# Padding small tables onto 512-byte lines, and moving four output stores from ScalarE's queue to SyncE's

## The chip, the cores and the metric

The kernel runs on one core of one Trainium2 chip. The metric is device time in microseconds (us). Five engines run their own instruction streams and meet at semaphores: TensorE (PE, matmuls; PEld is its weight load), VectorE (DVE), ScalarE (ACT), GpSimd (POOL) and SyncE (SP). SP, ACT and POOL can issue DMAs. In the profile SPq, ACTq and POOLq are the issuing instructions of these queues, and "Lnnn" is a line of the kernel's file.

## What is computed

The reference runs a recurrent retention layer (4 batches, 8 heads, 768 steps, head size 64) and feeds its output, seen as 3072 tokens of 512, to a two-layer network with a leaky ReLU whose slope is learned:

```python
for t in range(S):
    state = gamma[None, :, None, None] * state + np.einsum('bhd,bhe->bhde', k[:, :, t], v[:, :, t])
    y[:, :, t] = scale * np.einsum('bhd,bhde->bhe', q[:, :, t], state)
x = y.transpose(0, 2, 1, 3).reshape(B * S, H * D)
h = x @ w_in                                             # 3072 x 2048
g = np.maximum(h, 0.0) + alpha * np.minimum(h, 0.0)
out = g @ w_out                                          # 3072 x 512, float32
```

## The kernel before, in words

**Units and blocks.** The retention is done in chunks of 128 steps. A unit `i` is two chunks and half of the heads; there are 24 units. Four units make a block of 512 tokens, and there are six blocks, 0 to 5. Block n's retention gives the tile `xT[n]`; then `ffn1(n)` (L335, 64 matmuls of 512 columns) gives `gt`, and `ffn2(n)` (L375, 64 matmuls) gives the output.

**Life of a unit.** `load` (L118) brings k, q and v of the unit to SBUF, 256 KB each, on SP's queue, into tiles `ks`, `qs`, `vs`. `u_prep` multiplies k and q by decay factors from the table `tab` (L145, tile `kdq`) and casts v (L161, `vx`). For blocks 0 and 1 the transposed copy `kq` is made by PE and ACT (`u_turn`, L175 and L184); from block 2 on it is made by a transposing DMA on SP's queue (`u_flip`, L165). `u_visit` has the state update (L204 on PE, L223, L227 on DVE, L228 on POOL), the scores (L245 on PE) and the mask (L258 on DVE). `u_out` (L280, L295 on PE) gives the unit's output, which ACT copies into `xT` (L315).

**The two layers.** For each of 16 slices of 128 hidden features, `ffn1` runs four matmuls into a PSUM tile `hps`; ACT makes `hm` from it (L345) and DVE makes `gt` (L346). For block 1 the first slice is done in two halves of 256 columns. `ffn2` ends, for each of four row groups, with ACT's copy of PSUM to `os_sb` (L384) and a store of 256 KB to `out` (L388), issued by ACT. With `parts=4`, as for block 0, all four row groups end in the last quarter of `ffn2`. PSUM tiles of all kinds share eight buffers, given in turn.

**Order.** The program's order is written out by hand (`manual_schedule`): each engine runs its instructions in the order in which they stand in the code, and the generators of `ffn1` and `ffn2` are advanced with `tick` between steps of the units. Around the change the code reads as follows: `ffn2(0)` is advanced between the visits of units 4 to 7, `u_out(7)` stands between its second and third row group, then come the twelve loads of block 2 (units 8 to 11), then `ffn1(1)`, and inside it, for each unit i of block 2, the preparation, `u_flip(8+i)` and the three loads of unit 12+i. So SP's queue has: loads of units 8 to 11, flip 8, loads of unit 12, flip 9, loads of unit 13, and so on. ACT's queue has: `os` copy and store of row groups 0 and 1, the two `xT` copies of unit 7, `os` copy and store of row groups 2 and 3, then the `hm` of `ffn1(1)`.

**Counters.** The DMAs issued by SP and ACT, in the program's order, take eight completion counters in turn; a DMA whose counter was last used by an earlier DMA carries a wait until that one has landed. The wait stands in the issuing engine's queue.

**Addresses.** SBUF tiles are laid one after another in the order of the code, each rounded up to 32 bytes per partition. In the compiled program `tab` starts 128 bytes past a line of 512 bytes; its 208 bytes, the 768 of `mi`, the 4 of `warm` and the 64 of `oma` leave every tile from `win` on (all of `ks`, `qs`, `vs`, `kdq`, `kq`, `xT`, `gt`, `os`) 192 bytes past a 512-byte line. `gmat`, `alpha` and `spin` start 96 bytes past one.

Of the kernel before, what the change touches and what calls it, by code (L numbers as in the profile page):

```python
# [9 lines left out]
FP = mybir.dt.float32  # L10
F16 = mybir.dt.float16
# [7 lines left out]
def kernel(  # L19
# [10 lines left out]
    nc = tc.nc  # L30
    B, H, S, D = q.shape
    d_model, d_ff = moe_w_in.shape
    NFT = d_ff // 128
# [13 lines left out]
    NTAB = 4 * H + NP + 16  # L47
# [24 lines left out]
    sbp = ctx.enter_context(tc.tile_pool(name="sbp", bufs=1, space=bass.MemoryType.SB))  # L72
    psp = ctx.enter_context(tc.tile_pool(name="psp", bufs=1, space=bass.MemoryType.PSUM))
    ctx.enter_context(tc.manual_schedule())

    tab = sbp.tile([128, NTAB], FP, tag="tab", name="tab")
    mi = sbp.tile([128, 384], F16, tag="mi", name="mi")
    ident = mi[:, 0:128]
    masku = mi[:, 128:384].rearrange("p (s i) -> p s i", s=2)
    gmat = sbp.tile([128, NP, 128], FP, tag="gmat", name="gmat")  # L80
    alpha_sb = sbp.tile([NFT, 128], FP, tag="alpha", name="alpha")
    spin = sbp.tile([128, 512], F16, tag="spin", name="spin")
    warm = sbp.tile([128, 1], FP, tag="warm", name="warm")
    oma_sb = sbp.tile([128, NFT], FP, tag="oma", name="oma")
    w_in_all = sbp.tile([128, 4, d_ff], F16, tag="win", name="win")
    w_out_all = sbp.tile([128, NFT, d_model], F16, tag="wout", name="wout")

# [5 lines left out]
    def ps(name, dt=FP, n=512):  # L93
        return psp.tile([128, n], dt, tag="ps", bufs=8, name=name)
# [15 lines left out]
    def load(u, names="kqv"):  # L110
        t = staged.setdefault(u, {})
        for nm in names:
            src = srcs[nm]
            st = sbp.tile([128, H * D], FP, tag=f"{nm}s", bufs=8, name=f"{nm}s{u}")
            j, g = divmod(u, 2)
            b, c = divmod(2 * j, NCH)
            t[nm] = st
            ins = nc.sync.dma_start(  # L118
                out=st.rearrange("p (h x) -> p h x", h=H // 2),
                in_=src[  # L120
                    b, H // 2 * g : H // 2 * g + H // 2, C * c : C * c + 2 * C, :
                ].rearrange("h (p s) d -> p h (s d)", s=2),
            )
            if held:
                tc.add_manual_dep(
                    ins.ins,
                    held.pop().ins.name,
                    mybir.DependencyInfo(
                        mybir.DependencyClass.Sync, mybir.DependencyReason.DATA
                    ),  # L130
                    reason="loads of the second block after the weights",
                )
# [195 lines left out]
    def ffn1(n, early=0):  # L328
        gt = sbp.tile([128, NFT, TB], F16, tag="gt", bufs=2, name=f"gt{n}")
        gts[n] = gt  # L330
        hpss = {}

        def product(ft, lo, hi, hps=range(4)):
            for hp in hps:
                nc.tensor.matmul(  # L335
                    out=hpss[ft][:, lo:hi],
                    lhsT=w_in_all[:, hp, 128 * ft : 128 * ft + 128],
                    rhs=xT[n][:, hp, lo:hi],
                    start=(hp == 0),
                    stop=(hp == 3),  # L340
                )
                if hp == 3 and hi == TB:
                    hpt = hpss.pop(ft)
                    hm = sbp.tile([128, TB], FP, tag="hm", bufs=3, name="hm")
                    nc.scalar.activation(out=hm, in_=hpt, func=RELU, bias=0.0, scale=-1.0)  # L345
                    nc.vector.scalar_tensor_tensor(  # L346
                        out=gt[:, ft, :],
                        in0=hm,
                        scalar=oma_sb[:, ft : ft + 1],
                        in1=hpt,  # L350
                        op0=MULT,
                        op1=ADD,
                    )
                yield

        for ft in range(early):
            hpss[ft] = ps("hps")
            yield from product(ft, 0, TB // 2)
            yield from product(ft, TB // 2, TB, range(2))
        for ft in range(early):  # L360
            yield from product(ft, TB // 2, TB, range(2, 4))
        for ft in range(early, NFT):
            hpss[ft] = ps("hps")
            yield from product(ft, 0, TB)

    def ffn2(n, parts=1):
        gt = gts.pop(n)
        opss = {}
        step = NFT // parts
        for f0 in range(0, NFT, step):  # L370
            for tq in range(UB):
                if f0 == 0:
                    opss[tq] = ps("ops")
                for ft in range(f0, f0 + step):
                    nc.tensor.matmul(  # L375
                        out=opss[tq],
                        lhsT=gt[:, ft, 128 * tq : 128 * tq + 128],
                        rhs=w_out_all[:, ft, :],
                        start=(ft == 0),
                        stop=(ft == NFT - 1),  # L380
                    )
                    if ft == NFT - 1:
                        os_sb = sbp.tile([128, d_model], FP, tag="os", bufs=6, name="os")
                        nc.scalar.activation(  # L384
                            out=os_sb, in_=opss[tq], func=COPY, bias=0.0, scale=1.0
                        )
                        row = TB * n + 128 * tq
                        nc.scalar.dma_start(out=out[row : row + 128, :], in_=os_sb)  # L388
                    yield

    def tick(gen, m):
# [14 lines left out]
    for lh in range(2):  # L406
        z = slice(64 * lh, 64 * lh + 64)
        nc.gpsimd.tensor_copy(
            out=gmat[z, :, z],
            in_=tab[z, 4 * H : 4 * H + NP].unsqueeze(2).to_broadcast([64, NP, 64]),  # L410
# [16 lines left out]
    def masked(i):  # L427
# [60 lines left out]
        out=aps[:, 0:NFT], in_=alpha_sb, identity=tab[0:NFT, NTAB - 16 : NTAB]  # L488
    )
    nc.vector.tensor_scalar(  # L490
        out=oma_sb, in0=aps[:, 0:NFT], scalar1=-1.0, scalar2=1.0, op0=MULT, op1=ADD
# [9 lines left out]
    gen = ffn1(0, early=4)  # L501
# [7 lines left out]
    u_scale(4, 0)  # L509
    for _ in gen:  # L510
        pass
    gen = ffn2(0, parts=4)

    def u_visit(i):
        st[i] = u_state(i)
# [39 lines left out]
        pass  # L555
    for u in range(2 * UB, 3 * UB):
        load(u)
    gen = ffn1(1, early=1)

    for n in range(1, NBLK):  # L560
        more = n + 1 < NBLK
        u0 = UB * (n + 1)
        if n > 1:
            gen = ffn1(n)
        if more:
            for i in range(UB):
                tick(gen, 14)
                u_prep(u0 + i, nc.gpsimd)
                u_flip(u0 + i)
                if u0 + i + UB < NU:  # L570
                    load(u0 + i + UB)
        for _ in gen:
            pass
        gen = ffn2(n)
        if more:
            for i in range(UB):
                u = u0 + i
                tick(gen, 2)
                if i:
                    u_out(u - 1)  # L580
                u_visit(u)
                tick(gen, 12)
            u_out(u0 + UB - 1)
        for _ in gen:
            pass
# [30 lines left out]
```

## Time and profile before

| | us |
|---|---|
| median of three runs (lowest, highest) | 222.0 (220.98, 224.34) |
| the profiled execution, its own time | 222.42 |
| its span, first to last instruction | 220.6 |
| TensorE busy in the span | 209.0 (95%) |
| VectorE, ScalarE, GpSimd busy | 119.6, 100.9, 83.1 |

The page cuts the span into 40 slices of 5.5 us; a digit is the busy share of a slice in tenths. The granted clock is 0.996 of full speed. A chain of waits follows the work back from the last instruction to what released it. Times of single rows are counted from the span's start.

### The profile page before, as it was taken

The numbers are of one execution on the slowest core, as the hardware profiler recorded it, in microseconds if no ns is written. First come the engines' busy times: TensorE is split into PE (matmuls) and PEld (weight loads), VectorE is DVE, ScalarE is ACT, GpSimd is POOL, SyncE is SP. The second block draws the span as 40 slices with busy tenths as digits, with TensorE's granted clock in tenths as the row PEclk, the third lists the DMA queues.
The fourth block names the chain that finished last, engine by engine and source line by source line (L and its number), as shares of the span: only waits on it lengthen the run. The fifth ranks groups of instructions, "written<-read, shape, count | busy, mean of one in ns | idle before, by whom it ended". The sixth has DMA issues, their size and how long they took to land.

```text
span 220.6 us, 4964 instructions
## 1 busy us (share of the span) xinstructions
PE 209.0 (95%) x2043; PEld 104.3 (47%) x2043; DVE 119.6 (54%) x195; ACT 100.9 (46%) x185; POOL 83.1 (38%) x107
## 2 busy tenths in 40 slices
PE   7998997899599999999999999999999999999992
PEld 3456543454344455444455444555444555444440
DVE  2674794655009954178846088554288642388000
ACT  2583873334329523376233466232567222666121
POOL 3487204941990042990013990112980331000000
PEclk9999999999999999999999999999999999999998
DMA  6999999978999961499911499811482002100111
GB/s 171 300 221 167 174 242 293 232 138 235 312 250 305 295 180 51 107 270 229 255 51 51 113 251 293 203 51 62 133 103 40 22 35 91 48 0 1 51 68 74
DMA packets 62935, 34.02 MB, mean 154 GB/s; under 512 B 18736, under 2 KB 59840, under 8 KB 62912
## 3 DMA queue, kind: packets, MB, share of 16 engines
q1 hardware_dynamic: 54912, 23.08, 45.5%
q0 software_dynamic: 4224, 4.19, 12.3%
q10 hardware_dynamic: 3776, 6.43, 8.1%
q8 instruction: 16, 0.26, 0.5%
q14 instruction: 7, 0.06, 0.1%
HBM read 27.40 MB, written 6.29 MB: 153 GB/s over the span
## 4 chain that ended last, share of the span: by engine, by line
PE 73%; DMA 12%; POOL 4%; SPq 3%; DVE 3%; issue 2%; ACT 1%; ACTq 0%; POOLq 0%; DVEq 0%
PE ops L375 35%; PE hps L335 28%; DMA qs<-in_q_dram 5%; DMA win<-in_moe_w_in_dram 4%; SPq L118 3%; PE yps L295 3%; DMA vs<-in_v_dram 3%; PE stp L204 2%; POOL tg L228 2%; POOL kdq L145 2%; PE yps L280 2%; PE sca L245 1%; DVE m L258 1%; POOL win L418 1%; PE scb L245 1%
## 5 line engine op out<-in xcount | busy, mean ns | idle before, releaser
L346 DVE SCALAR_TENSOR_TENSOR gt<-hm,oma,hps 128x512 f16<-128x512 f32 x96 | 69.1, 745 | 41.5 <-ACT hm L345 34.9
L375 PE MATMUL ops<-wout,gt 128*128 128x512 f16 x384 | 89.3, 380 | 0.0
L335 PE MATMUL hps<-xT,win 128*128 128x512 f16 (+1 forms) x404 | 84.6, 368 | 2.7 <-ACT xT L315 2.6
L345 ACT ACTIVATE hm<-hps 128x512 f32<-128x512 f32 x96 | 56.5, 597 | 24.3 <-PE hps L335 21.9
L335 PEld LDWEIGHTS <-win 128*128 128x128 f16 x404 | 39.4, 98 | 46.4 <-issue 3.3
L228 POOL TENSOR_TENSOR tg<-ss,gmat 128x256 f16<-128x256 f32 x32 | 23.2, 727 | 82.4 <-DVE ss L227 82.4
L375 PEld LDWEIGHTS <-gt 128*128 128x128 f16 x384 | 35.3, 98 | 39.9
L315 ACT ACTIVATE xT<-yps 128x256 f16<-128x256 f32 x48 | 18.5, 453 | 35.2 <-PE yps L295 28.4
L145 POOL TENSOR_TENSOR kdq<-qs,tab 128x512 f16<-128x512 f32 x24 | 25.4, 1059 | 17.4 <-DMA qs<-in_q_dram 17.4
L384 ACT ACTIVATE os<-ops 128x512 f32<-128x512 f32 x24 | 14.3, 597 | 37.5 <-PE ops L375 33.9
L227 DVE TENSOR_TENSOR ss<-tg,stp 128x256 f32<-128x256 f16 x32 | 13.2, 415 | 25.2 <-PE stp L204 25.2
L258 DVE TENSOR_TENSOR m<-sca,mi 128x512 f16<-128x512 f32 x24 | 16.4, 683 | 1.5 <-PE scb L245 1.1
L145 POOL TENSOR_TENSOR kdq<-ks,tab 128x512 f16<-128x512 f32 x16 | 16.7, 1045 | 0.0
L184 ACT ACTIVATE kq<-trb 128x512 f16<-128x512 f16 (+1 forms) x11 | 8.7, 790 | 16.9 <-PE trb L175 16.8
L258 DVE TENSOR_TENSOR m<-scb,mi 128x512 f16<-128x512 f32 x24 | 16.3, 680 | 0.0
L161 POOL CAST vx<-vs 128x512 f16<-128x512 f32 x20 | 12.7, 635 | 0.0
L204 PE MATMUL stp<-vx,kdq 64*64 64x128 f16 x320 | 9.7, 219 | 0.4 <-ACT vx L159 0.4
L295 PE MATMUL yps<-m,vx 64*64 64x128 f16 x384 | 10.0, 222 | 0.0
L100 PE MATMUL kps<-spin 128*128 128x512 f16 x22 | 8.5, 510 | 1.5 <-DVE spin L403 1.5
L245 PE MATMUL sca<-kq 64*64 64x128 f16 x192 | 9.7, 217 | 0.2
L245 PE MATMUL scb<-kq 64*64 64x128 f16 x192 | 9.7, 219 | 0.0
L223 DVE TENSOR_TENSOR tg<-stp,gmat 128x256 f16<-128x256 f32 x8 | 3.4, 423 | 11.0 <-PE stp L204 11.0
(25 smaller groups left out, 67.5 us busy)
## 6 DMA issues: line engine op xcount, KB each, us to landing
ks<-in_k_dram SPq DMA_DIRECT2D x24, 256.0 KB, 4.4
qs<-in_q_dram SPq DMA_DIRECT2D x24, 256.0 KB, 4.9
vs<-in_v_dram SPq DMA_DIRECT2D x24, 256.0 KB, 5.3
out_dram<-os ACTq DMA_DIRECT2D x24, 256.0 KB, 2.0
win<-in_moe_w_in_dram POOLq DMA_DIRECT2D x4, 512.0 KB, 7.1
wout<-in_moe_w_out_dram POOLq DMA_DIRECT2D x4, 512.0 KB, 9.1
kq<-kdq SPq DMA_TRANSPOSE x16, 4.5
mi<-mi_const ACTq DMA_DIRECT2D x1, 96.0 KB, 2.9
```

Of the source, the lines that this page charges most:

```text
L145: (eng or (nc.vector, nc.gpsimd)[a]).tensor_tensor(out=prepped[i][0][:, a], in0=staged[i]["kq"[a]].rearrange("p (h s d) -> p s h d", s=2, ...
L204: nc.tensor.matmul(out=stps[hf][64 * lh : 64 * lh + 64, 128 * r : 128 * r + 128], lhsT=kdu[z, 0, s, 2 * r + lh, :], rhs=vx[z, 2 * r : 2 * ...
L228: nc.gpsimd.tensor_tensor(out=tgs[u + 1][:, gs, :], in0=new, in1=gmat[:, gs, :], op=MULT)
L245: nc.tensor.matmul(out=scs[lh][z, c0 : c0 + 128], lhsT=kqv[y, 0, s, r, z], rhs=kqv[y, 1, :, r, z], start=True, stop=True,)
L258: nc.vector.tensor_tensor(out=m2, in0=scs[lh].rearrange("p (s r i) -> p s r i", s=2, r=2), in1=masku.unsqueeze(2).to_broadcast([128, 2, 2, ...
L295: nc.tensor.matmul(out=ypss[hf][64 * lh : 64 * lh + 64, 128 * r : 128 * r + 128], lhsT=vx[z, 2 * r + lh, s, :], rhs=m2s[lh][z, s, r, :], s ...
L315: nc.scalar.activation(out=xT[n][:, 2 * g : 2 * g + 2, c0 : c0 + C].rearrange("p a (i s) -> p a s i", s=2), in_=ypss[hf][:, 0:256].rearran ...
L335: nc.tensor.matmul(out=hpss[ft][:, lo:hi], lhsT=w_in_all[:, hp, 128 * ft : 128 * ft + 128], rhs=xT[n][:, hp, lo:hi], start=(hp == 0), stop ...
L345: nc.scalar.activation(out=hm, in_=hpt, func=RELU, bias=0.0, scale=-1.0)
L346: nc.vector.scalar_tensor_tensor(out=gt[:, ft, :], in0=hm, scalar=oma_sb[:, ft : ft + 1], in1=hpt, op0=MULT, op1=ADD,)
L375: nc.tensor.matmul(out=opss[tq], lhsT=gt[:, ft, 128 * tq : 128 * tq + 128], rhs=w_out_all[:, ft, :], start=(ft == 0), stop=(ft == NFT - 1),)
L384: nc.scalar.activation(out=os_sb, in_=opss[tq], func=COPY, bias=0.0, scale=1.0)
```

## The change

Four small tiles are allocated larger, and a slice of each is used as before: `tab` 52 to 96 floats a partition, `mi` 384 to 512 half floats, `warm` 1 to 64 floats, `oma` 16 to 64 floats. With these sizes `tab` ends on a 512-byte line, and each tile after it starts on one, except `oma`, which starts 256 bytes past a line.

The four stores of block 0 are no longer issued by ACT. `ffn2` keeps their rows and tiles in a list, and SP issues them, after the twelve loads of block 2 and ahead of flip 8. The stores of the other blocks stay with ACT.

```diff
-    tab = sbp.tile([128, NTAB], FP, tag="tab", name="tab")
-    mi = sbp.tile([128, 384], F16, tag="mi", name="mi")
+    tab = sbp.tile([128, 96], FP, tag="tab", name="tab")[:, 0:NTAB]
+    mi = sbp.tile([128, 512], F16, tag="mi", name="mi")[:, 0:384]
...
-    warm = sbp.tile([128, 1], FP, tag="warm", name="warm")
-    oma_sb = sbp.tile([128, NFT], FP, tag="oma", name="oma")
+    warm = sbp.tile([128, 64], FP, tag="warm", name="warm")[:, 0:1]
+    oma_sb = sbp.tile([128, 64], FP, tag="oma", name="oma")[:, 0:NFT]
...
-    def ffn2(n, parts=1):
+    def ffn2(n, parts=1, late=None):
...
                         row = TB * n + 128 * tq
-                        nc.scalar.dma_start(out=out[row : row + 128, :], in_=os_sb)
+                        if late is None:
+                            nc.scalar.dma_start(out=out[row : row + 128, :], in_=os_sb)
+                        else:
+                            late.append((row, os_sb))
...
-    gen = ffn2(0, parts=4)
+    stores = []
+    gen = ffn2(0, parts=4, late=stores)
...
     for u in range(2 * UB, 3 * UB):
         load(u)
+    for row, os_sb in stores:
+        nc.sync.dma_start(out=out[row : row + 128, :], in_=os_sb)
     gen = ffn1(1, early=1)
```

## The prediction, made before the change was run

> **What bounds the kernel now.** I read the page first, then the chain of waits in order of time, then the timelines of ACT, PE and SP where the chain leaves PE. The page says that PE is the bound:
>
> ```profile
> PE   7998997899599999999999999999999999999992
> ...
> DMA  6999999978999961499911499811482002100111
> ...
> PE 73%; DMA 12%; POOL 4%; SPq 3%; DVE 3%; issue 2%; ACT 1%; ACTq 0%; POOLq 0%; DVEq 0%
> ```
>
> After the first four slices the PE row has one true dip, the 5 in slice 11, which is 55 to 60.5 us: the end of block 0's second layer, where the changed stores stand. The DMA row is full there. In the chain this is the piece that is not PE:
>
> ```profile
> 57.96 0.53 SPq L118
> 58.49 0.05 issue
> 58.58 6.13 DMA vs<-in_v_dram
> 64.79 0.34 ACTq L388
> 65.23 0.61 ACT hm L345
> 65.86 0.76 DVE gt L346
> 66.66 7.07 PE hps L335 x32
> ```
>
> A load of block 2 (v of unit 11, 6.13 us) ends, and only then does ACT issue a store of block 0 (L388) and go on. ACT's timeline shows that all four stores do this:
>
> ```profile
> 56.41 0.36 ACTq L388 DMA_DIRECT2D out_dram<-os  x1
> 56.82 0.60 ACT L384 ACTIVATE os<-ops 128x512 f32<-128x512 f32 x1 [2.28 <-DMA qs<-in_q_dram]
> 58.56 0.41 ACTq L388 DMA_DIRECT2D out_dram<-os  x1
> 59.02 0.76 ACT L315 ACTIVATE xT<-yps 128x256 f16<-128x256 f32 x2 [1.59 <-DMA vs<-in_v_dram]
> 59.62 0.60 ACT L384 ACTIVATE os<-ops 128x512 f32<-128x512 f32 x1
> 61.11 0.34 ACTq L388 DMA_DIRECT2D out_dram<-os  x1
> 61.50 0.60 ACT L384 ACTIVATE os<-ops 128x512 f32<-128x512 f32 x1 [1.27 <-PE hps L335]
> 64.79 0.34 ACTq L388 DMA_DIRECT2D out_dram<-os  x1
> ```
>
> The landings of the trace's completion counters explain these times: the counters that the four stores need were last used by the loads q9, v9, v10 and v11, which landed at 56.34, 58.48, 61.04 and 64.71, each 0.07 to 0.08 us before the store. So ACT is held by loads that it does not need, and behind the stores in its queue stand the two copies of `xT` for unit 7. PE waits for them:
>
> ```profile
> 56.91 0.49 PE L335 MATMUL hps<-xT,win 128*128 128x256 f16 x3
> 59.83 0.49 PE L335 MATMUL hps<-xT,win 128*128 128x256 f16 x3 [2.43 <-ACT xT L315]
> ```
>
> Single matmul starts are 0.11 us apart here; from the third (57.12) to the fourth (59.83) are 2.70, so 2.59 are lost. At 66.66 another 0.25 go (starts 0.47 apart, not 0.22), for a PSUM buffer that the late `hm` and `gt` give back. The sum is checked another way: from the first `hps` matmul of block 1 (56.91) to its first `ops` matmul (73.57) are 16.66 us; the chain gives 13.81 for the same work in each of blocks 2 to 5. 16.66 - 13.81 = **2.85 us**.
>
> **The stores, step by step.** ACT loses four issues (0.36 + 0.41 + 0.34 + 0.34 = 1.45 us) and four waits. Without them: `os` 0 ends at 54.55; `os` 1 can follow (its matmuls end near 55.1); PE's L280 group of unit 7 ends near 55.8, so the `xT` copies (0.76) end near 56.7. PE asks for them at 57.23. The 2.59 go entirely, with about 0.5 us of cover. Then `os` 2 and 3 (0.60 each) end near 58; the first `hm` needs its `hps` at about 57.9, and then ACT (0.60) and DVE (0.75) each do a slice in less than PE's 0.86. The PSUM wait of 0.25 goes too. What is late next is nothing up to PE's own rate.
>
> What SP gains: the four stores stand behind load v11, whose issue ends at 59.33, and ahead of flip 8. Their data are ready by then (58). Their turn of counters becomes that of q9, v9, k10 and q10, which landed at 56.34, 58.48, 59.34 and 60.19, so the fourth can hold SP until 60.2. Flip 8 then has the counter of v10 (61.04). An unhindered store issue took 0.34 us on ACT; loads on SP in this stretch took from 0.46 to 2.22 us each:
>
> ```profile
> 55.27 2.22 SPq L118 DMA_DIRECT2D ks<-in_k_dram  x1
> 57.59 0.90 SPq L118 DMA_DIRECT2D qs<-in_q_dram  x1
> 58.58 0.75 SPq L118 DMA_DIRECT2D vs<-in_v_dram  x1
> 59.43 2.94 SPq L165 DMA_TRANSPOSE kq<-kdq  x1
> ```
>
> So four issues cost SP 1.4 to 8.9 us. I take 0.46 each, the commonest load issue from 51 to 54 us, 1.8 in all: flip 8 starts at 61.1 instead of 59.43, 1.7 later. Its data also stand behind four stores instead of two (stores 0 and 1 had landed at 61.71 and 63.97, before flip 8 at 66.62). A store is 128 packets of 2 KB at 86 ns over 16 engines, 0.7 us; two are 1.4. Flip 8 lands at 68.3 to 69.7.
>
> Who waits for it: the scores of unit 8, at 74.34 now and at 71.5 after the gain. Cover is about 2 us, against 7.7 now. Flips 9, 10 and 11 landed at 70.66, 74.13 and 77.61 and are needed 4.2 us apart, so their cover is larger. Loads of units 12 to 15 are behind too, but POOL takes them only at 88.47, and the last landed near 80.7. The `hm` that move forward overlap POOL's preparations (55.9 to 66.2); the same overlap stands in block 2 (94 to 99), where PE keeps 13.81.
>
> **The padding.** It adds and removes no instruction and no byte. What can change is the time of a packet or of an operand's access. No trace here has an aligned tile to compare, so I take the packet records by size (medians): 4 bytes 9 ns, 208 bytes 16, 512 bytes 29 (27 in the fastest tenth), 768 bytes 36, 2048 bytes 86. A line through the ends, 9 ns + 0.0375 ns a byte, gives 17, 28 and 38 for the middle ones, so a packet that crosses a 512-byte line (all but 4 and 208 bytes) costs no more than bytes and a fixed share say; only a cost in proportion to the bytes could hide in the slope. I take **0**. The other end: if 512-byte packets lost 5 ns of 27 to splitting, loads would be up to 16% shorter. Two places could use that. In block 1, PE lost 0.55 and 1.03 us, the excess of two gaps between matmul starts, at unit 4:
>
> ```profile
> 34.86 0.40 PE L175 MATMUL trb<-mi,kdq 128*128 128x128 f16 x4 [0.39 <-DVE kdq L145]
> 36.12 0.40 PE L175 MATMUL trb<-mi,kdq 128*128 128x128 f16 x4 [0.87 <-POOL kdq L145]
> ```
>
> These wait for k4 and q4 (landed 34.09 and 34.95), whose loads wait for the weights (27.99): 1.58 at most. At the start, the load of q3 lands at 12.94 and POOL follows; 16% of the 11 us since the first packet are 1.7. Together at most 3.3 us. As a loss, engines that now meet on the same phase of a line could slow; PE's matmuls have 216 ns apart and slack behind them, so I bound it at +1 us, the size of the third such wait (1.06, at 41.11, where DVE and POOL work at once).
>
> The Trainium skill speaks for the large end (DMA: Bandwidth & Descriptors, "How a descriptor splits into AXI transactions"): a descriptor that does not start on a 256-byte boundary fetches from the boundary below, so by its count 512 bytes from 192 past would read 22 beats instead of 16. The line of packet times above leaves no room for that, and the loads write SBUF rather than read it, but no aligned row is here to decide. The same page ("Issuing engines are not separate DMA queues") holds that the issuing engine matters only for its issue time; by that, the move would be worth at most the 1.45 us of issues. The trace differs: ACT's gaps end with landings.
>
> **The sum.** 222.42 - 2.85 + 0 = 219.6 for the profiled execution. The median of the runs shown is 0.4 lower, so the forecast is 222.0 - 2.85 = **219.2 us**, 1.3% faster.
>
> **The rivals.**
> 1. *Padding shortens transfers too* (0.20). For: the DMA row is full from 28 to 38 and 52 to 78 us, and the mean 512-byte packet is 31 ns, not 27. Against: the line above. Time: 219.2 less 0.7 to 3.3, so 215.9 to 218.5.
> 2. *Flip 8 takes the place of the removed wait* (0.13). SP issues of about 1.2 us each would spend the cover of 2 us, and PE loses part of the 2.85: 220.3 to 222.0. This case also holds the change not doing what it says: ACT held by some other wait, which would leave 222.0.
> 3. *Slower than before* (0.10). The stores' issues each take as long as the longest load issue, 2.22 us: SP reaches flip 8 at 68.2 instead of 59.43, and flip 8 lands 8.8 us later plus 1.4 for two stores, at 76.8. PE, ready at 71.5, loses 5.3 us and gains 2.85: 224.5. It decides from the point where flip 8 is more than 7.7 us late (66.62 to 74.34). The later flips come 3.5 to 4 us apart and are needed 4.2 apart, so the loss is paid once. A loss of 1 us from the layout would add to it.
>
> **Chances.** The forecast itself (218.5 to 220.3) has 0.57. The range 216.6 to 222.2 leaves out the best third of rival 1 and rival 3. A difference of 2%, 4.4 us, is about what a measurement of this kernel can tell from no change. Faster by more than that (below 217.6) needs most of rival 1: 0.13. Slower (above 226.4) needs rival 3 and more: 0.04. Within: 0.83.
>
> **What would show it.** Right: no DMA among ACT's releasers from 53 to 66 us; slice 11 of the PE row at 9; block 1's first layer at 13.8 to 14.0 us; four store rows on SP's timeline between 59 and 62; flip 8 landed before the scores of unit 8. Rival 1: 512-byte packets below 27 ns, and the waits at 34.86 and 36.12 shorter. Rivals 2 and 3: PE idle before L245 near 71.5, released by `kq`. The forecast is wrong if anything but `xT` and PSUM held PE at 57 to 67 us, or if the layout moves a rate that I took as fixed.

## The result and the profile after

The changed kernel takes **218.84 us** (median of four runs, 218.2 to 218.98) against 222.14 for the kernel before beside it (220.98 to 224.34): ratio 0.986, 95% interval 0.982 to 0.991. The forecast was 219.2. The profiled executions go from 222.42 us (span 220.6) to 218.76 (span 217.0). Ratios here and below leave out disturbed runs and refer to runs of the kernel before on the same occasion, whose medians lay between 222.1 and 224.0, so two experiments are best compared by their own times.

From the page of the changed kernel, the PE and DMA rows of the 40 slices and the chain's shares:

```profile
PE   7898998899999999999999999999999999999992
...
DMA  6999999976999993799512699702650111100111
...
PE 91%; DVE 3%; ACT 2%; POOL 1%; issue 0%; DVEq 0%
```

The dip of slice 11 is gone, and the chain that ended last no longer shows a DMA (12% before). Of these 12% only the load of v11, 6.13 us or 3%, stood where the stores were; the rest were loads before 35 us, which the chain followed then and does not follow now, so their share is not time gained. In order of time, the chain around the change reads:

```profile
55.23 1.29 PE ops L375 x6
56.53 13.82 PE hps L335 x68
70.35 0.43 PE ops L375 x2
```

Block 1's first layer is now one piece of 13.82 us. Before, ACT, a store's issue and a load of 6.13 us stood in it, and it took 16.66. ACT's timeline of the changed kernel at the same place:

```profile
53.41 0.60 ACT L384 ACTIVATE os<-ops 128x512 f32<-128x512 f32 x1 [1.29 <-PE ops L375]
54.27 0.60 ACT L384 ACTIVATE os<-ops 128x512 f32<-128x512 f32 x1 [0.27 <-PE ops L375]
55.06 0.77 ACT L315 ACTIVATE xT<-yps 128x256 f16<-128x256 f32 x2 [0.19 <-PE yps L295]
55.70 0.60 ACT L384 ACTIVATE os<-ops 128x512 f32<-128x512 f32 x1
56.57 0.60 ACT L384 ACTIVATE os<-ops 128x512 f32<-128x512 f32 x1 [0.27 <-PE ops L375]
57.44 0.60 ACT L345 ACTIVATE hm<-hps 128x512 f32<-128x512 f32 x1 [0.28 <-PE hps L335]
```

Every wait of ACT in this stretch is for PE, none over 1.29 us. The copies of `xT` end at 55.83, before PE asks. SP's timeline has what was moved:

```profile
58.01 0.61 SPq L118 DMA_DIRECT2D vs<-in_v_dram  x1
58.71 2.17 SPq L563 DMA_DIRECT2D out_dram<-os  x4
60.98 2.50 SPq L165 DMA_TRANSPOSE kq<-kdq  x1
```

Four store issues take 0.54 us each, waits included, and flip 8 starts 1.55 us later than before (59.43). By the completion counters it landed at 66.05, and PE's scores of unit 8 started at 70.96: 4.9 us of cover. Flips 9, 10 and 11 landed 4.5, 3.2 and 3.8 us ahead of theirs.

The account of the two profiled spans, 3.63 us in all: 2.84 in block 1's first layer (first `hps` matmul to first `ops` matmul, 56.91 to 73.57 before, 56.37 to 70.19 after); 0.54 ahead of it (56.91 to 56.37), nearly all of it at unit 4, where PE's two losses of 0.55 and 1.03 became one of 1.08; 0.25 behind 70.19. At the start nothing was gained in these two profiles: the load of q3 landed 0.65 us earlier (12.29 instead of 12.94), but the first `hps` matmul started at 18.53 as before (18.54), because it now waited for the first weights, `win`, which landed at 18.48. The page of the changed kernel has this wait, 0.5 us of idle time, in the row of the weight loads:

```profile
L335 PEld LDWEIGHTS <-win 128*128 128x128 f16 x404 | 39.4, 98 | 43.9 <-DMA win<-in_moe_w_in_dram 0.5
```

### The profile page after: what moved, and what is told of

The parts are those of the page before. It is cut to its first block, busy times and chain, and to the rows that moved or that the text cites. A ratio compares the mean times of both kernels' runs of the same rounds, so it can differ in the third digit from the quotient of the medians.

```text
span 217.0 us, 4963 instructions
## 1 busy us (share of the span) xinstructions
PE 208.2 (96%) x2043; PEld 104.4 (48%) x2043; DVE 121.8 (56%) x195; ACT 101.2 (47%) x185; POOL 83.6 (39%) x107
## 4 chain that ended last, share of the span: by engine, by line
PE 91%; DVE 3%; ACT 2%; POOL 1%; issue 0%; DVEq 0%
PE ops L375 38%; PE hps L335 38%; PE yps L295 3%; PE kps L100 3%; PE stp L204 2%; PE yps L280 2%; PE sca L245 2%; PE trb L175 2%; DVE m L258 1%; DVE kdq L145 1%; ACT kq L184 1%; PE scb L245 1%; POOL tg L228 1%; DVE ss L227 1%; ACT vx L159 0%
## 5 line engine op out<-in xcount | busy, mean ns | idle before, releaser
L346 DVE SCALAR_TENSOR_TENSOR gt<-hm,oma,hps 128x512 f16<-128x512 f32 x96 | 70.5, 747 | 36.3 <-ACT hm L345 27.8
L145 DVE TENSOR_TENSOR kdq<-ks,tab 128x512 f16<-128x512 f32 x8 | 7.0, 879 | 4.9 <-DMA ks<-in_k_dram 4.9
(25 smaller groups left out, 70.5 us busy)
```

The source lines that it names most:

```text
L145: (eng or (nc.vector, nc.gpsimd)[a]).tensor_tensor(out=prepped[i][0][:, a], in0=staged[i]["kq"[a]].rearrange("p (h s d) -> p s h d", s=2, ...
L346: nc.vector.scalar_tensor_tensor(out=gt[:, ft, :], in0=hm, scalar=oma_sb[:, ft : ft + 1], in1=hpt, op0=MULT, op1=ADD,)
```

## The experiments

Two questions: is the gain the stores' wait alone, and what held the stores; and what does the padding do?

**The stores without the padding.** The four sizes of the tables go back; the stores stay on SP.

```diff
-    tab = sbp.tile([128, 96], FP, tag="tab", name="tab")[:, 0:NTAB]
-    mi = sbp.tile([128, 512], F16, tag="mi", name="mi")[:, 0:384]
+    tab = sbp.tile([128, NTAB], FP, tag="tab", name="tab")
+    mi = sbp.tile([128, 384], F16, tag="mi", name="mi")
...
```

> The stores on SP's queue, without the padding (tiles from win on stay 192 bytes past a 512-byte line). Theory (the stores' move alone is worth PE's two waits, 2.59 + 0.25 us): 222.1 - 2.85 = 219.3 us; no gap over 0.2 us between matmul starts from 56 to 74 us; 512-byte packets as before (median 29 ns, mean 31); PE still loses 0.55 and 1.03 at unit 4. Rival (part of the gain came from loads that land earlier through the padding): 220 to 221 us, with a part of the wait for xT left.

Measured: 219.2 us, ratio 0.984 (0.978 to 0.990). In the chain, block 1's first layer is one piece, as long as in the changed kernel:

```profile
56.85 13.82 PE hps L335 x68
```

No matmul start is more than 0.1 us late between 56 and 74 us. The packets are no faster than in the kernel before (median 32 ns and mean 32.1, against 29 and 31.4). The theory holds, its 219.3 met within 0.1: the two waits of PE go with the stores alone. PE loses 0.51 and 0.67 at unit 4, where 0.55 and 1.03 were expected.

**The padding without the move.** The kernel before with the four padded sizes, stores on ACT.

```diff
-    tab = sbp.tile([128, NTAB], FP, tag="tab", name="tab")
-    mi = sbp.tile([128, 384], F16, tag="mi", name="mi")
+    tab = sbp.tile([128, 96], FP, tag="tab", name="tab")[:, 0:NTAB]
+    mi = sbp.tile([128, 512], F16, tag="mi", name="mi")[:, 0:384]
...
```

> The padding alone, block 0's stores on ACT as before. Theory (the padding shortens the loads' packets, median 29 to 27 ns, mean 31 to 28; that takes 0.5 us from PE's waits at unit 4, and, since the stores on ACT still wait for the loads q9, v9, v10, v11, lets xT come as much earlier as v9 lands, 1.4 us): 222.1 - 0.5 - 1.4 = 220.2 us, and PE's gap before the fourth hps matmul of block 1 shrinks from 2.6 to about 1.2 us. Rival (the padding does nothing; the faster packets after the change came from the stores being out of the loads' way): 222 us, packets of 29 to 31 ns.

Measured: 220.45 us, ratio 0.9895 (0.984 to 0.995). ACT's timeline of this kernel, and then PE's:

```profile
55.92 0.36 ACTq L388 DMA_DIRECT2D out_dram<-os  x1
...
56.96 0.34 ACTq L388 DMA_DIRECT2D out_dram<-os  x1
57.35 0.76 ACT L315 ACTIVATE xT<-yps 128x256 f16<-128x256 f32 x2 [0.42 <-ACT os L384]
```

```profile
58.16 1.14 PE L335 MATMUL hps<-xT,win 128*128 128x256 f16 x7 [1.77 <-ACT xT L315]
```

The first store still comes just after q9 lands (55.85 by the counters); v9 has landed (56.60) before the second, which follows its `os` copy at once. So `xT` comes 1.7 us earlier than before (59.02), and PE still waits for it: 1.93 us by its matmul starts, instead of 2.59; the 0.25 for PSUM is gone. So the padding alone does work, through the loads: 512-byte packets take 27 ns in the median and 28.3 in the mean. The rival falls. The size of the PE wait was missed (1.2 expected), because the block's end, from which ACT wants to go on, came 1 us earlier as well (PE's third `hps` matmul at 56.12 instead of 57.12).

The two parts overlap: both take from the wait for `xT`, so their separate gains must not be added.

**Which boundary counts.** One more tile is widened so that all tiles from `win` on start 256 bytes past a 512-byte line (128 floats), or 32 bytes past one (72 floats).

```diff
-    oma_sb = sbp.tile([128, 64], FP, tag="oma", name="oma")[:, 0:NFT]
+    oma_sb = sbp.tile([128, 128], FP, tag="oma", name="oma")[:, 0:NFT]
```

In the second kernel the 128 is 72.

> As the changed kernel, but oma is 128 floats wide, so that every tile from win on starts 256 bytes past a 512-byte line. If a packet pays for each 512-byte line that it crosses: packets of 512 bytes as before the change (median 29 ns, mean 31), and PE's loss at unit 4 near 1.6 us, 219.3 us. If it pays for a start off a 256-byte boundary: packets as in the changed kernel (median 27, mean 28), 218.8 us.

> As the changed kernel, but oma is 72 floats wide, so that every tile from win on starts 32 bytes past a 512-byte line, on no 64-byte boundary. If only crossing a boundary costs, whatever the offset: packets as before the change (median 29, mean 31), 219.3 us. If an offset below 64 bytes costs more: median over 31 ns and 219.6 us or more. If the padding has no part in the packets' time: 27 to 28 ns, 218.8 us.

Read directly from the packet records, for the 36,864 packets of 512 bytes of each kernel:

| start past a 512-byte line | median, mean ns | share up to 28 ns |
|---|---|---|
| 192 (kernel before) | 29, 31.4 | 47% |
| 0 (changed kernel) | 27, 28.2 | 96% |
| 256 | 27, 28.4 | 96% |
| 32 | 29, 31.0 | 50% |

The times: 218.78 us at 256 (ratio 0.982, 0.975 to 0.989) and 219.58 at 32 (0.985, 0.978 to 0.992). So a start on a 512-byte line is not needed, 256 bytes past one does as well, and 32 bytes off are no worse than 192. A boundary of 256 bytes fits the four rows; one of 128 would fit them too, since no start at 128 was run. One part of the expectation missed: at 256 PE's loss at unit 4 was 1.21 us, no less than with the stores moved and slow packets (about 1.2 in both runs).

**The price of the padding once the stores are moved.** The changed kernel and the one without padding again, on the same chip.

> The changed kernel once more, beside the next run on the same chip, to price the padding where the stores are already on SP. Theory (padding gives packets of 27 ns instead of 29 to 32, which shortens only the start, where PE waits for data, and unit 4's waits): 0.3 to 0.6 us faster than the kernel without padding, first hps near 18.4 us, unit 4's loss near 1.1. Rival (nothing is bound by those packets once the stores are moved): the two within 0.2 us.

> The stores on SP's queue without the padding, the other half of the pair. Theory: 219.2 us, 0.3 to 0.6 slower than the changed kernel, first hps near 18.7 us, unit 4's loss 1.2 to 1.6. Rival: the two within 0.2 us.

Measured: 218.75 us with the padding (218.43 to 219.93; ratio 0.980, 0.976 to 0.985), 219.69 without (218.54 to 219.74; ratio 0.982, 0.978 to 0.986). The medians are 0.9 us apart, more than the 0.3 to 0.6 expected, but the two intervals overlap; PE's loss at unit 4 was 1.2 us in both. The order is that of the two earlier runs (218.84 and 219.2, which were not side by side). That the packets take less time is clearer than what it is worth. SP's queue in the page, with the padding and without:

```profile
q1 hardware_dynamic: 55488, 24.12, 44.4%
```

```profile
q1 hardware_dynamic: 55488, 24.12, 47.7%
```

The columns are packets, MB and the time of the packets as a share of 16 engines' span: the same packets and bytes, 3.3 points less time. The first `hps` matmul of block 0, behind the first loads, starts at 18.05 with the padding and at 19.29 without. That difference, 1.24 us, is nearly all of the 1.30 between the two profiled spans, but much of it can be chance: over all profiles of this study the first `hps` starts at 17.67 to 18.69 on 512-byte lines (eight profiles, median 18.2; three of the changed kernel alone differ by 0.76), at 18.72 with tiles at 256 bytes, and at 18.54 to 19.29 off both (five, median 18.7).

**Another queue than SP.** The kernel before, without padding, with block 0's stores issued by GpSimd where ACT issued them.

```diff
-                        nc.scalar.dma_start(out=out[row : row + 128, :], in_=os_sb)
+                        (nc.scalar if n else nc.gpsimd).dma_start(out=out[row : row + 128, :], in_=os_sb)
```

> The kernel before, without the padding, with block 0's four stores issued by GpSimd in place: at the same points of the program, through other completion counters, which nothing holds. Theory (ACT was held by counters last used by loads, not by the stores' data or full rings): POOL issues each store within 1 us of its os copy (near 54.9, 55.7, 57.5 and 58.5), ACT's timeline has no gap before xT of unit 7, PE's 2.6 are gone, about 219.3 us; the preparation of unit 8 on POOL starts near 58.5 instead of 55.9 and flip 8 lands near 69, in time. Rival (a store issued among block 2's loads is held by the loads' own traffic): POOL's store rows come as late as ACT's did (56.4 to 64.8), the preparations start after 65, the flips land after 74, and PE waits for kq: 222 us or more.

Measured: 219.03 us, ratio 0.984 (0.979 to 0.990). POOL's timeline:

```profile
55.78 1.78 POOL L388 DMA_DIRECT2D out_dram<-os  x3
57.89 0.54 POOL L388 DMA_DIRECT2D out_dram<-os  x1 [0.32 <-ACT os L384]
58.44 1.05 POOL L145 TENSOR_TENSOR kdq<-ks,tab 128x512 f16<-128x512 f32 x1
```

Behind POOL's own work, which ended at 55.8, the stores issue one after another among the same loads, with no wait but that for the last `os`. So it was not the loads' traffic that held them on ACT. The trace of the kernel before shows directly that it was the counters: just ahead of each of ACT's four stores stands a wait of ACT for the counter that q9, v9, v10 or v11 had used last. PE's gaps are gone, and 2.5 us of delay for the preparation of unit 8 cost nothing.

**ACT again, but later.** The changed kernel with the late stores issued by ACT.

```diff
-        nc.sync.dma_start(out=out[row : row + 128, :], in_=os_sb)
+        nc.scalar.dma_start(out=out[row : row + 128, :], in_=os_sb)
```

> As the changed kernel, with the four late stores issued by ACT instead of SP, still after all of ffn2(0) in the program. Their counters are then those of q9, v9, k10 and q10, as on SP, which land by 59.3. Theory (the harm was that stores stood ahead of the xT copies, not that ACT issued them): xT on time; the first hm waits until about 59.8 instead of 57.4, but PE has PSUM buffers until 63.3 and the first gt ends near 61.2, so nothing is lost: 218.8 us. Rival (any wait of ACT there costs PE, so the stores had to leave its queue): PE loses 1 to 3 us between 57 and 70, 220 to 222 us.

Measured: 222.81 us, ratio 1.001 (0.997 to 1.005): the whole gain is lost, and the theory falls. ACT's timeline, and then a table of windows (from and to, length, busy time and instructions of PE, weight loads, DVE, ACT and POOL, then granted clock, DMA share, GB/s):

```profile
57.83 7.06 ACTq L563 DMA_DIRECT2D out_dram<-os  x4
65.00 1.58 ACT L345 ACTIVATE hm<-hps 128x512 f32<-128x512 f32 x3 [7.75 <-DMA out_dram<-os]
```

```profile
57.00:63.00 6.00, 6.00 (x32) 2.90 (x30) 0.00 (x0) 0.25 (x1) 6.00 (x8) 1.00 1.14 259
63.00:66.40 3.40, 0.53 (x3) 0.13 (x2) 0.78 (x2) 1.41 (x3) 2.72 (x4) 1.00 1.09 350
66.40:70.50 4.10, 4.07 (x12) 1.51 (x12) 4.10 (x7) 3.73 (x8) 0.00 (x0) 0.58 1.17 337
```

`xT` was on time (55.91). But the four stores held ACT until 64.9. The counters were not those that I had expected: the stores got those of k10, v10, q11 and flip 8, which lands at 64.48. So the counters are not handed out in the order of the code, as I had described it, for flip 8 stands behind all four stores there. The kernel before shows the same: in the code its four stores stand ahead of the loads q9, v9, v10 and v11 whose counters they waited for. What sets the order is not shown. PE ran out of PSUM buffers at 63.4 and stood for 3.06 us; the third window then shows a granted clock of 0.58. The lower clock is not needed for the loss: of the ten runs, the five with a mean clock of 0.996 or more have a median of 221.9 us, as the kernel before has in such runs, and the five with 0.984 to 0.992 have 223.6. So it is not enough that the stores stand behind `xT`; what ACT does next waits just as PE does. Whether the move behind `xT` with free counters would do was not tried.

**How much cover flip 8 has.** Each store on SP is cut into four of 32 rows.

```diff
-        nc.sync.dma_start(out=out[row : row + 128, :], in_=os_sb)
+        for r in range(0, 128, 32):
+            nc.sync.dma_start(out=out[row + r : row + r + 32, :], in_=os_sb[r : r + 32, :])
```

> As the changed kernel, but each of the four stores on SP's queue is cut into four of 32 rows: 16 issues of some 0.54 us, 8.7 us in place of 2.2, so flip 8 starts near 67.4 instead of 61. It measures how much cover flip 8 has. Theory (PE needs kq of unit 8 at 71.1, and a flip lands 3 to 5 us after its start): flip 8 lands at 70.5 to 73 and PE loses 0 to 2 us before the scores of unit 8: 218.8 to 220.8 us; the later flips are late by less. Rival of the prediction (stores on SP put the flips late enough to lose all of the gain): 222 us or more.

Measured: 220.1 us, ratio 0.989 (0.984 to 0.994). SP's timeline, and the two rows of PE's that lost time:

```profile
56.60 7.60 SPq L564 DMA_DIRECT2D out_dram<-os  x16
64.30 1.33 SPq L165 DMA_TRANSPOSE kq<-kdq  x1
...
71.23 5.11 SPq L165 DMA_TRANSPOSE kq<-kdq  x1
```

```profile
79.57 0.24 PE L245 MATMUL sca<-kq 64*64 64x128 f16 x1 [0.55 <-DMA kq<-kdq]
...
84.61 0.24 PE L245 MATMUL sca<-kq 64*64 64x128 f16 x1 [0.70 <-DMA kq<-kdq]
```

The time came out inside the expected range, but at another place. Flip 8 is in time (landed at 67.11, where 70.5 to 73 was expected); flip 10, whose issue took 5.11 us (1.46 in the changed kernel), and flip 11 behind it are late, and PE loses 0.71 and 0.86 us by its matmul starts. Why that one issue took so long stays open. What it shows for the change: 5.4 us more of SP's time for the stores (7.60 instead of 2.17), in sixteen pieces, cost 1.3 us of the gain, and the late flip need not be the first one.

**A version that beats both.** With the stores gone, PE's two largest losses are the 1.08 us at unit 4 and 1.06 us near 40 us, where it waits for unit 5's k. The second is tried here. DVE scales it behind unit 4's masks while POOL scales q. The preparation is put ahead:

```diff
     u_turn(4, (0, 1))
+    u_prep(5)
     tick(gen, 6)
     u_visit(4)
-    u_prep(5)
```

> As the changed kernel, with the preparation of unit 5 put ahead of the visit of unit 4 (its loads landed near 36, and DVE is idle from 36 to 37.7). Theory (the 1.06 us that PE loses at 40.6 is unit 5's k, scaled by DVE only after unit 4's masks and at the same time as POOL scales q): that gap goes, 217.8 us. Rival (the scaling then delays unit 4's state and masks, and PE waits there instead): 218.8 us or more, with a new gap before unit 4's yps or stp.

> The changed kernel with unit 5's preparation ahead of unit 4's visit, once more, beside the changed kernel on the same chip. Theory (it takes the 1.06 us that PE loses at 40 us and gives back some 0.4 in small gaps at 44 to 50): 0.6 to 0.8 us faster than the changed kernel, near 218.0. Rival (the gap removed is paid back elsewhere): the two within 0.2 us.

> The changed kernel, the other half of the pair: 218.8 us by both; 0.6 to 0.8 us slower than the one with the early preparation by the theory, within 0.2 us of it by the rival.

Measured: 218.03 us first (ratio 0.980, 0.976 to 0.984). Then, beside the changed kernel on one chip, 217.34 (0.976, 0.971 to 0.981) against 218.47 (0.982, 0.977 to 0.987). PE's transposes of unit 5, in the version with the early preparation and then in the changed kernel beside it:

```profile
38.41 0.61 PE L175 MATMUL trb<-mi,kdq 128*128 128x128 f16 x8
```

```profile
39.92 0.62 PE L175 MATMUL trb<-mi,kdq 128*128 128x128 f16 x8 [0.90 <-DVE kdq L145]
```

The wait is gone, and in the second profile of this version nothing is paid back (in the first, 0.17 and 0.27 us at 44.8 and 49.2). The difference of the pair, 1.1 us, is the size of the wait removed and more than the 0.6 to 0.8 expected, though the intervals of the two ratios overlap.

## Why the prediction came out as it did

- **The sum.** Forecast 222.0 - 2.85 = 219.2, measured 218.84. The term that carried it was right to 0.01 in the profiles: 16.66 - 13.82 = 2.84 us of block 1's first layer. The kernel with the stores' move alone, which is the forecast with a padding that does nothing, took 219.2 us and the second time 219.69. The base was partly luck: 222.0 is the median of three runs, and that of all 49 runs of the kernel before in this study is 222.83, from which the same saving gives 220.0, still inside the range.
- **What held ACT.** Right. ACT's waits for the counters explain the starts before the change, and in the GpSimd run, with other counters, no load held a store. I wrote ahead of the prediction that the counters are taken in the program's order, and that is wrong, as the run with ACT issuing late showed. The prediction took the counters of the kernel before from the trace, so this did no harm there, and those it gave for the changed kernel (last used by q9, v9, k10 and q10) came out. In block 1 the move gave 2.84 us, and with ACT as the issuer the whole gain was lost. The rule of the Trainium skill that I weighed against this ("DMA: Bandwidth & Descriptors", section "Issuing engines are not separate DMA queues") is that another issuing engine saves only the issue time. By it the move would have given at most 1.45 us, so it does not cover a queue that is held by a counter.
- **SP's side.** 0.46 us taken per store issue, 0.54 measured, between the bounds of 0.34 and 2.22; flip 8 started at 60.98 where 61.1 was forecast. Its landing, 68.3 to 69.7 forecast, was 66.05: the term mis-sized is the transfers ahead of it, since v11 landed at 62.32 and not 64.71, with no stores among the loads and faster packets. The larger part came from the stores: from the issue of load k8 to the landing of v11 took 15.7 us before, 13.9 and 14.0 with the move alone, 13.3 with both. Cover was 4.9 us, not 2. The last load of units 12 to 15 had landed at 81.53 before the change, not near 80.7; nothing rests on it. The row of four stores on SP, named as between 59 and 62, is at 58.71 to 60.88.
- **The padding.** Wrong step: "I take 0". The line through packet sizes was drawn from medians and the fastest tenth, and the fastest packets do not change at all (27 ns at any offset). The cost lies in the other half: before, only 47% of the 512-byte packets take up to 28 ns, after, 96%, and the mean falls by 3.2 ns (10%). The mean of 31 ns stood in the prediction and was set aside. In time it is worth some 0.6 us with the stores moved (median 218.75 of 16 runs against 219.35 of 12 without padding), just under the low end of rival 1, which had a chance of 0.20. Its size is uncertain, since the two sets of runs overlap (218.1 to 220.0 and 218.5 to 219.7). The end of 3.3 us was far too large: PE's start waits for the first weights too, which landed at 18.48 in the changed kernel, so an earlier q3 gained nothing there.
- **The boundary.** Starts at 0 and 256 bytes agree, and so do 32 and 192. That fits the 256-byte boundary that the Trainium skill names ("How a descriptor splits into AXI transactions", same page). Its count of beats does not fit: by an estimate from it, a packet from 192 takes 22 beats against 16 and would be dearer by over a third of its data time, and one from 32 takes only 17. The traces have half the packets unchanged at both, and means of 31.4 and 31.0 ns against 28.2.
- **Rivals 2 and 3.** Neither happened. The cut stores came near rival 2 (220.1 us, of the range 220.3 to 222.0), by flips 10 and 11 and not by flip 8; that a later flip could be late while the first was in time had not been foreseen.

## What to carry to other kernels

When an engine's DMA row starts just behind the landing of a transfer that it does not need, look for a completion counter that the two share, and move the DMA to a queue that has nothing urgent behind it; moving it later on the same queue can leave the wait where it was. Price such a wait at the engine that is the bound, by comparing the same stage in another block (16.66 against 13.81 us here). For packets, look at the share of slow ones and not at the median: starts on a 256-byte boundary of SBUF cost 832 padded bytes a partition here.

## What the runs showed of the hardware that I had not expected

**The offset in SBUF changes only part of the packets.** At 192 and 32 bytes past a line the fastest 512-byte packets take the same 27 ns as aligned ones, while half of them take 29 to 40. What decides which is not shown.

**A wait of PE can cost more than itself.** In the run with ACT issuing late, PE stood 3.06 us, up to 66.43, and the trace then has a granted clock of half speed from 67.02 to 70.44, 3.4 us; matmuls of 512 columns started 0.43 us apart instead of 0.216, and some 1.7 us were lost behind the wait. The page's clock row shows it in slice 13:

```profile
PEclk9999999999996999999999999999999999999998
```

The profiled kernel before (2.59 us of waiting) has no such drop, nor has the one with the padding alone (1.93). But of 49 single runs of the kernel before in this study, 23 report a mean clock of 0.984 to 0.992 (median 224.1 us) and 26 one of 0.996 or more (221.9); the changed kernel's 16 runs all report 0.996 or more. One drop of 3.4 us to half speed takes 0.008 from the mean over 220 us, and the run of this trace reports 0.990; so the low values have the size of one such drop, or of two for the lowest. That it came behind the wait for `xT` in the kernel before is argued from this, not shown: no trace of one of its low runs is there. If so, the change also removes an extra loss that the kernel before had in about half of its runs. The wait alone probably does not decide it, since five of the ten runs with ACT issuing late report 0.996 or more.

The Trainium skill ("TensorE: Matmul & The Clock Gate", "What's actually happening") has the clock halved after an idle window of about 3.4 us on a free-running timer. Here a wait of 3.06 us was followed by the drop, and the half clock lasted 3.41. By an estimate with that window, the one that ended at 67.02 began at 63.61 and held 0.6 us of matmuls, so it was not idle throughout.
